# Sixty-four rows of a weight matrix through GpSimd's queue, and a reordered end of the last attention heads, in a decode kernel on one Trainium2 core

## The chip, the cores and the metric

The kernel runs on one core of one Trainium2 chip. The metric is device time in microseconds (us), the median of repeated executions. Kernels are compared only within the same rounds.

Ratios are the mean time of one kernel's fast runs over that of the other's of the same rounds, so a ratio is not quite the ratio of the medians that are quoted. The brackets hold a 95% interval.

## The reference

One decode step for 4 sequences: layer norm of x, then attention over a window of 2,048 cached keys in 32 heads of width 192, plus a gated feed-forward block on the same normalised input.

```python
W = min(4096, max(256, Sk // 4))                       # 2048
q = (xn @ wq).reshape(4, 1, 32, 192)                   # D = 640
scores = einsum("bhqd,bhkd->bhqk", q, k[last W]) * 192**-0.5
o = einsum("bhqk,bhkd->bhqd", softmax(scores), v[last W])
h = silu(xn @ w1) * (xn @ w3)                          # F = 1536
out = x + o.reshape(4, 1, 6144) @ wo + h @ w2
```

All data are bfloat16. K and V of the window are 201 of the 223 MB that have to be read once.

## The kernel before

Every head is one 3 MB K load and one 3 MB V load on SyncE's DMA queue. VectorE multiplies K by q, TensorE sums the products (`adder`), VectorE reduces them, a short chain over all engines gives the exponentials, VectorE spreads them into `z`, and TensorE multiplies z by V (`pv`). The result, divided by the sums and transposed, is `oT`, which TensorE multiplies by wo.

Two places matter here. The first is the load of w1, 640 rows of 1,536. The first 512 rows fill 128 partitions evenly. The next 64 rows are cut in halves, one half row for each partition, so that all 16 DMA engines share them (16 completion increments in the trace of before, 46.15 to 46.74 us, which I take as one an engine). The last 64 rows come as four small pieces into 12 partitions each.

```python
    KM, PH, LE, LI = KC - 1, P // 2, 3, 4               # 4, 64, 3, 4
    LP, LF, LB = LE * LI, CT + LE * LI, KM * P + PH      # 12, 44, 576
...
    def w1_load():
        w = B_w1
        wt = fpool.tile([P, FH + F], BF16, tag="w", name="w1")
        we = wopool.tile([LF, 2 * F], BF16, tag="wo", name="w1e")
        nc.gpsimd.memset(we[:], 0.0)
        nc.gpsimd.memset(wt[0:LF, FH:], 0.0)
        nc.sync.dma_start(out=wt[:, 0:FM], in_=w[0:KM * P, :].rearrange("(p kc) n -> p (kc n)", kc=KM))
        nc.sync.dma_start(out=wt[:, FM:FH], in_=w[KM * P:LB, :].rearrange("r (h n) -> (r h) n", h=2))
...
    def w1_low(n):                                      # four small pieces, 12 partitions each
        if n < 2:
            b0 = LB + n * 2 * LP
            nc.sync.dma_start(out=we[n * CT:n * CT + LP, :],
                              in_=w[b0:b0 + 2 * LP, :].rearrange("(i e s) n -> e i (s n)", e=LE, s=2))
...
```

The small pieces show the idea that the change extends. Their outer dimension is 3, and in the trace of before the first one has, after an increment soon after its issue, three completion increments (54.37 to 54.44 us) and not 16. I read this as three DMA engines: the piece gives those three more work, and the other 13 none.

The second place is the end. Slots of a schedule set the program order. Head 31 (the last, `H - 1`) has its chain and value product behind all of head 30's.

```python
    ends = {H - 2: (NU - 1, NU), H - 1: (NU + 3, NU + 4)}
    for h in range(H):
        u0, ul = h * GQ, h * GQ + GQ - 1
...
        for u in range(u0, ul + 1):
            add(u, 1, mult, u)
            add(u + 1, 2, adder, u)
            add(u + 1, 8, reduce_quarter, u)
        add(ul + 1, 9, chain_lmax, h)
        add(ul + 2, 3, chain_tr, h)
        add(ul + 2, 4, chain_gmax, h)
        add(ul + 3, 3, chain_bc, h)
        add(ul + 3, 4, chain_z, h)
        add(ul + 4, 5, ge_tot, h)
...
        v, m = ends.get(h, (u0 + L, u0 + L + 1))
        add(v, 7, pv, h)
        add(m, 7, ge_sum, h)
```

Of the kernel before, what the change touches and what calls it, by code (L numbers as in the profile page):

```python
# [10 lines left out]
FP32 = mybir.dt.float32  # L11
BF16 = mybir.dt.bfloat16
# [38 lines left out]
def kernel(  # L51
# [19 lines left out]
    nc = tc.nc  # L71
    P = 128
    B, Sq, D = A_x.shape
    _, H, Sk, Dh = A_k_cache.shape
    W = min(4096, max(256, Sk // 4))
    F = B_w1.shape[1]
# [129 lines left out]
    KM, PH, LE, LI = KC - 1, P // 2, 3, 4  # L206
    LP, LF, LB = LE * LI, CT + LE * LI, KM * P + PH
    assert D - LB == 5 * LP + LI and F % LE == 0
    xm = ppool.tile([B, 2, PH, 2], BF16, tag="pr", name="xm")
    nc.gpsimd.memset(xm[:], 0.0)  # L210
    for i in range(2):
        nc.vector.tensor_copy(out=xm[:, i, :, i], in_=xn[:, KM * P:LB])
    xe = ppool.tile([B, 3 + LE, LF], BF16, tag="pr", name="xe")
# [7 lines left out]
    for e in range(LE):  # L221
        nc.vector.tensor_copy(out=xe[:, 3 + e, CT + e * LI:CT + (e + 1) * LI], in_=xn[:, LB + 5 * LP:D])
    NX = KM + 2
    xw_ps = ps_t.tile([P, NX + 3 + LE, B], BF16, tag="t", name="xw_ps")
    for kc in range(KM):
        nc.tensor.transpose(out=xw_ps[:, kc, :], in_=xn[:, kc:KM * P:KM], identity=idb[0:B, 0:B])
    for i in range(2):
        nc.tensor.transpose(out=xw_ps[:, KM + i, :], in_=xm[:, i].rearrange("b r h -> b (r h)"), identity=idb[0:B, 0:B])
    for i in range(3 + LE):
        nc.tensor.transpose(out=xw_ps[0:LF, NX + i, :], in_=xe[:, i, :], identity=idb[0:B, 0:B])  # L230
    xw = const.tile([P, NX, NREP, B], BF16, name="xw")
    nc.vector.tensor_copy(out=xw[:], in_=xw_ps[:, 0:NX, :].unsqueeze(2).to_broadcast([P, NX, NREP, B]))
    xl = const.tile([LF, 3 + LE, NREP, B], BF16, name="xl")
    nc.vector.tensor_copy(out=xl[:], in_=xw_ps[0:LF, NX:, :].unsqueeze(2).to_broadcast([LF, 3 + LE, NREP, B]))

# [148 lines left out]
    FM, FH = KM * F, KM * F + F // 2  # L384

    def w1_load():
        w = B_w1
        wt = fpool.tile([P, FH + F], BF16, tag="w", name="w1")
        we = wopool.tile([LF, 2 * F], BF16, tag="wo", name="w1e")
        nc.gpsimd.memset(we[:], 0.0)  # L390
        nc.gpsimd.memset(wt[0:LF, FH:], 0.0)
        nc.sync.dma_start(out=wt[:, 0:FM], in_=w[0:KM * P, :].rearrange("(p kc) n -> p (kc n)", kc=KM))
        nc.sync.dma_start(out=wt[:, FM:FH], in_=w[KM * P:LB, :].rearrange("r (h n) -> (r h) n", h=2))
        ffn["w1"], ffn["w1e"] = wt, we

    def w1_low(n):
        w, wt, we = B_w1, ffn["w1"], ffn["w1e"]
        if n < 2:
            b0 = LB + n * 2 * LP
            nc.sync.dma_start(out=we[n * CT:n * CT + LP, :],  # L400
                              in_=w[b0:b0 + 2 * LP, :].rearrange("(i e s) n -> e i (s n)", e=LE, s=2))
        elif n == 2:
            nc.sync.dma_start(out=wt[0:LP, FH:FH + F], in_=w[LB + 4 * LP:LB + 5 * LP, :].rearrange("(i e) n -> e i n", e=LE))
        else:
            nc.sync.dma_start(out=wt[CT:LF, FH:FH + F // LE], in_=w[LB + 5 * LP:D, :].rearrange("i (e n) -> e i n", e=LE))

    def w1_in():
# [12 lines left out]
        for w in range(HG):  # L420
            c0 = FM + (w % 2) * FW
            mm(w, xw[:, KM + w // 2], wt[:, c0:c0 + FW])
        for i in range(2):
            for w in range(HG):
                mm(w, xl[:, i], we[:, i * F + w * FW:i * F + (w + 1) * FW])
        for w in range(HG):
            mm(w, xl[:, 2], wt[0:LF, FH + w * FW:FH + (w + 1) * FW])
        FE = F // LE
        for e in range(LE):
            for w in range(HG):  # L430
                c0, c1 = max(e * FE, w * FW), min((e + 1) * FE, (w + 1) * FW)
                if c0 < c1:
                    mm(w, xl[:, 3 + e], wt[0:LF, FH + c0 - e * FE:FH + c1 - e * FE], c0 - w * FW)
# [3 lines left out]
    def w3_load():  # L437
        wt = fpool.tile([P, KC, F], BF16, tag="w", name="w3")
        nc.sync.dma_start(out=wt[:].rearrange("p k n -> p (k n)"), in_=B_w3.rearrange("(p kc) n -> p (kc n)", kc=KC))
        ffn["w3"] = wt  # L440
# [33 lines left out]
    def add(slot, phase, fn, *args):  # L474
        sched[slot].append((phase, len(sched[slot]), fn, args))
# [3 lines left out]
    ends = {H - 2: (NU - 1, NU), H - 1: (NU + 3, NU + 4)}  # L479
    for h in range(H):  # L480
# [5 lines left out]
        for u in range(u0, ul + 1):  # L486
            add(u, 1, mult, u)
            add(u + 1, 2, adder, u)
            add(u + 1, 8, reduce_quarter, u)
        add(ul + 1, 9, chain_lmax, h)  # L490
        add(ul + 2, 3, chain_tr, h)
        add(ul + 2, 4, chain_gmax, h)
        add(ul + 3, 3, chain_bc, h)
        add(ul + 3, 4, chain_z, h)
        add(ul + 4, 5, ge_tot, h)
        if h % HG == HG - 1:
            add(ul + 4, 9, ge_rec, h // HG)
# [3 lines left out]
        if h % HG == HG - 1:  # L501
            add(m + 1, 0, ge_turn, h // HG)
    e = ends[H - 1][1] + 1
# [25 lines left out]
    add(e - 1, 8, ffn_out, 0)  # L529
# [44 lines left out]
```

## Time and profile before

| | before |
|---|---|
| time | 525.76 us (525.65 to 525.87, 3 runs) |
| span of the profiled run, mean granted clock | 523.8 us, 0.892 |
| bytes on the loads' queue | 222.96 MB |
| TensorE, VectorE busy | 69%, 65% |
| last w2 load landed | 520.75 us |

The first fence is from the profile page of before: the mean busy share of the DMA engines in 40 slices (in tenths), what they moved in GB/s, the queue of the loads, and the chain that ended last by engine.

```profile
DMA  9999999999999999999999999999999999999996
GB/s 389 422 443 425 433 431 432 428 433 432 430 435 428 437 418 446 424 437 426 434 434 429 432 434 429 435 427 435 425 437 434 427 437 431 430 434 425 441 418 275
...
q1 hardware_dynamic: 11868, 222.96, 99.2%
...
DMA 60%; PE 20%; DVE 15%; ACT 3%; issue 1%; SPq 1%
```

A share near 1.00 alone proves little: it counts time in which a packet was open. From 100 to 480 us the share is 1.00 at 432 GB/s. A packet of 24,576 bytes, one partition's part of a K or V load, takes 912 ns.

The end, from the timeline of TensorE of before (start and length in us, engine, line, operation, tiles, count; in brackets the idle time before it and what ended that):

```profile
513.30 2.71 PE L340 MATMUL o_ps<-vt,z 128*8 128x384 bf16 x32 [0.24 <-DVE z L332]
...
519.21 0.98 PE L264 MATMUL acc<-wo_t,oT 128*4 128x320 bf16 x12 [0.47 <-DMA wo_t<-in_A_wo_dram]
520.38 0.71 PE L264 MATMUL acc<-w,hT 128*4 128x320 bf16 x8 [0.19 <-DMA w<-in_B_w_dram]
```

The last two groups of products wait for loads, so the kernel ends with its DMA. The last w2 load has 16 completion increments, as many as there are DMA engines. Taken as one an engine, they show when each engine came to its end:

```
before, engine ends against 520.75 us: -3.2 -3.2 -3.0 -2.3 -1.9 -0.8 -0.8 -0.4 -0.3 -0.3 -0.3 -0.3 -0.3 -0.2 -0.1 0.0
mean of the 16: 519.68 us
```

Five engines are done 2 to 3 us early. Perfect balance would end all of them at their mean, 519.7 us, 1.1 us sooner. By this estimate that is all that balancing alone can win.

### The profile page before, as it was taken

The numbers are of one execution on the slowest core, as the hardware profiler recorded it, in microseconds if no ns is written. First come the engines' busy times: TensorE is split into PE (matmuls) and PEld (weight loads), VectorE is DVE, ScalarE is ACT, GpSimd is POOL, SyncE is SP. The second block draws the span as 40 slices with busy tenths as digits, with TensorE's granted clock in tenths as the row PEclk, the third lists the DMA queues.
The fourth block names the chain that finished last, engine by engine and source line by source line (L and its number), as shares of the span: only waits on it lengthen the run. The fifth ranks groups of instructions, "written<-read, shape, count | busy, mean of one in ns | idle before, by whom it ended". The sixth has DMA issues, their size and how long they took to land.

```text
span 523.8 us, 4820 instructions
## 1 busy us (share of the span) xinstructions
PE 361.8 (69%) x2336; PEld 75.9 (14%) x1643; DVE 340.9 (65%) x413; ACT 55.8 (11%) x176; POOL 5.6 (1%) x12
## 2 busy tenths in 40 slices
PE   0965866887668776667547768586686876675685
PEld 0100111121111111111111111111111111111122
DVE  3268853687656767577646877466667766667671
ACT  2111111111001110101100111001101110011111
POOL 4000000000000000000000000000000000000000
PEclk9979886898878998789997988889878898889988
DMA  9999999999999999999999999999999999999996
GB/s 389 422 443 425 433 431 432 428 433 432 430 435 428 437 418 446 424 437 426 434 434 429 432 434 429 435 427 435 425 437 434 427 437 431 430 434 425 441 418 275
DMA packets 11904, 223.26 MB, mean 426 GB/s; under 512 B 1332, under 2 KB 1608, under 8 KB 3052
## 3 DMA queue, kind: packets, MB, share of 16 engines
q1 hardware_dynamic: 11868, 222.96, 99.2%
q8 instruction: 15, 0.25, 0.2%
q14 instruction: 5, 0.04, 0.0%
q10 hardware_dynamic: 16, 0.01, 0.0%
HBM read 222.96 MB, written 0.01 MB: 426 GB/s over the span
## 4 chain that ended last, share of the span: by engine, by line
DMA 60%; PE 20%; DVE 15%; ACT 3%; issue 1%; SPq 1%
DMA kt<-in_A_k_cache_dram 44%; PE ps L288 11%; DMA w<-in_B_w_dram 11%; DVE pr L277 10%; DMA vt<-in_A_v_cache_dram 5%; PE po L361 4%; PE qps L243 3%; DVE sc L296 2%; ACT ex L324 1%; DVE z L332 1%; DMA x_sb<-in_A_x_dram 1%; PE mt L318 1%; ACT L324 0%; ACT negm L321 0%; PE mt L305 0%
## 5 line engine op out<-in xcount | busy, mean ns | idle before, releaser
L288 PE MATMUL ps<-pr,idb 128*128 128x512 bf16 x768 | 214.7, 422 | 137.6 <-DVE pr L277 137.5
L277 DVE TENSOR_TENSOR pr<-kt,qbc 128x3072 bf16<-128x3072 bf16 x128 | 223.5, 1746 | 104.0 <-DMA kt<-in_A_k_cache_dram 104.0
L296 DVE TENSOR_REDUCE sc<-ps 128x16 f32<-128x512 f32 x128 | 87.1, 681 | 2.7 <-PE ps L288 2.6
L340 PE MATMUL o_ps<-vt,z 128*8 128x384 bf16 x1024 | 60.5, 380 | 0.2 <-DVE z L332 0.2
L361 PE MATMUL po<-o_sb,sel_w 128*32 128x192 f32 x128 | 49.2, 518 | 0.6 <-ACT o_sb L343 0.6
L340 PEld LDWEIGHTS <-z 128*8 128x8 bf16 x1024 | 26.2, 95 | 98.8 <-issue 89.2
L332 DVE TENSOR_TENSOR z<-ex,mask_b 128x256 bf16<-128x256 bf16 x32 | 13.5, 423 | 38.6 <-ACT ex L324 38.6
L343 ACT COPY o_sb<-o_ps 128x384 f32<-128x384 f32 x32 | 15.3, 478 | 196.9 <-PE o_ps L340 196.9
L313 ACT ACTIVATE gneg<-gmax 1x128 f32<-1x128 f32 x32 | 9.8, 308 | 162.8 <-DVE gmax L310 162.8
L305 PEld LDWEIGHTS mt<-idf,lmax 128*1 128x1 f32 x32 | 3.2, 101 | 127.5 <-issue 125.5
L361 PEld LDWEIGHTS po<-o_sb,sel_w 128*32 128x32 f32 x128 | 13.8, 130 | 29.4 <-issue 27.9
L288 PEld LDWEIGHTS <-idb 128*128 128x128 bf16 x124 | 12.0, 97 | 39.3 <-issue 32.8
L318 PEld LDWEIGHTS mt<-ones_ff,gneg 1*128 1x128 f32 x64 | 9.6, 186 | 47.1 <-issue 43.7
L243 PE MATMUL qps<-wt,xnT 128*128 128x512 bf16 x59 | 14.9, 412 | 0.1
L318 PE MATMUL mt<-ones_ff,gneg 1*128 1x1 f32 x64 | 12.3, 259 | 0.7 <-ACT gneg L313 0.7
L321 ACT COPY negm<-mt 128x1 f32<-128x1 f32 x32 | 5.1, 159 | 70.4 <-PE mt L318 70.4
L310 DVE TENSOR_REDUCE gmax<-mt 1x4 f32<-1x128 f32 x32 | 8.8, 274 | 5.8 <-PE mt L305 5.8
L348 PEld LDWEIGHTS po<-rsum,tot_w 128*32 128x32 f32 x64 | 4.4, 108 | 51.5 <-ACT ex L324 35.4
L249 DVE CAST qbc<-qps 128x512 bf16<-128x512 f32 x6 | 3.8, 684 | 11.7 <-PE qps L243 11.7
L324 ACT ACTIVATE ex<-sc,negm 128x64 bf16<-128x64 f32 x32 | 11.1, 348 | 1.0
L305 PE MATMUL mt<-idf,lmax 128*1 128x128 f32 x32 | 10.9, 340 | 0.0
L199 PE MATMUL xnT_ps<-idb,xn 4*128 4x4 bf16 x5 | 0.4, 178 | 13.4 <-DVE xn L194 13.4
(74 smaller groups left out, 84.4 us busy)
## 6 DMA issues: line engine op xcount, KB each, us to landing
kt<-in_A_k_cache_dram SPq DMA_DIRECT2D x32, 3072.0 KB, 19.1
vt<-in_A_v_cache_dram SPq DMA_DIRECT2D x32, 3072.0 KB, 25.5
wo_t<-in_A_wo_dram SPq DMA_DIRECT2D x8, 960.0 KB, 20.7
wt<-in_A_wq_dram SPq DMA_DIRECT2D x2, 3072.0 KB
w<-in_B_w_dram SPq DMA_DIRECT2D x1, 1920.0 KB
wt<-in_A_wq_dram SPq DMA_DIRECT2D x1, 1536.0 KB, 19.5
w<-in_B_w_dram SPq DMA_DIRECT2D x1, 1536.0 KB
w<-in_B_w_dram SPq DMA_DIRECT2D x2, 640.0 KB
```

The source lines that it names most:

```text
L243: nc.tensor.matmul(qp[:], lhsT=xnT[:, kc].rearrange("p a b -> p (a b)"), rhs=wq_rows[kc][:, (c0 + i) * QC:(c0 + i + 1) * QC], start=(kc == ...
L277: nc.vector.tensor_tensor(out=pr[:], in0=kts[h][:, g * JQ:(g + 1) * JQ, :], in1=qbc[:, h * Dh:(h + 1) * Dh].unsqueeze(1).to_broadcast([P, ...
L288: nc.tensor.matmul(ps[:], lhsT=idb[:], rhs=pr[:, :, kk * DD:(kk + 1) * DD], start=(kk == 0), stop=(kk == NK - 1))
L296: nc.vector.tensor_reduce(out=scs[h][:, g * JQ:(g + 1) * JQ], in_=pss.pop(u)[:], axis=AX.X, op=ALU.add)
L305: nc.tensor.transpose(out=mt[0:1, 0:P], in_=chs[h][0][:], identity=idf[:])
L313: nc.scalar.activation(out=gneg[:], in_=gmax[:].unsqueeze(1).to_broadcast([1, PB, B]), func=ACTF.Copy, scale=-SCALE)
L318: nc.tensor.matmul(mt[:, P:P + 1], lhsT=gneg[:].rearrange("o p b -> o (p b)"), rhs=ones_ff[:], start=True, stop=True)
L324: nc.scalar.activation(out=ex[:], in_=scs.pop(h)[:], func=ACTF.Exp, bias=negm[:, 0:1], scale=SCALE, accum_out=rsum[:])
L332: nc.vector.tensor_tensor(out=z[:], in0=ex[:].unsqueeze(2).to_broadcast([P, NJ, B]), in1=mask_b[:].unsqueeze(1).to_broadcast([P, NJ, B]), ...
L340: nc.tensor.matmul(o_ps[c * CT:c * CT + 2 * B, :], lhsT=z[:, 2 * jj:2 * jj + 2, :], rhs=vt[:, 2 * jj:2 * jj + 2, :], start=(jj < 4), stop= ...
L343: nc.scalar.copy(out=o_sb[:], in_=o_ps[:])
L361: nc.tensor.matmul(po[sl, 0:Dh], lhsT=sel_w[:, par].rearrange("p a b -> p (a b)"), rhs=o_sb[:, par * Dh:(par + 1) * Dh].rearrange("p (r i) ...
```

## The change

Its intent has two parts.

- Loads: the 64 half rows no longer burden all engines. 24 rows and 40 rows are issued on GpSimd's queue as transfers with an outer dimension of 2, meant for one pair of engines each. Tiny transfers of 4, 1 and 7 rows (`skip`) are meant to move the place where GpSimd's queue takes its next engine, so that the pairs are engines 4 and 5, then 7 and 8. The destinations are partitions 16 to 23 and 60 to 67. Both the effect of the tiny transfers and the fit of these partitions to these engines were assumed: no trace had shown either.
- Tail: head 31's sums, largest score and exponentials stand ahead of head 30's value product where they can, and 25 matmuls whose results nobody reads fill TensorE's idle times.

```diff
-    LP, LF, LB = LE * LI, CT + LE * LI, KM * P + PH
+    LP, LF, LB = LE * LI, 68, KM * P
+    PA, PZ = 16, LF - GP                      # SA, SB, GP = 3, 5, 8
...
+    def skip(k):
+        t = const.tile([k, CT], BF16, name=f"skip{k}")
+        n = CT if k > 1 else CT - 1
+        nc.gpsimd.dma_start(out=t[:, 0:n], in_=B_w1[0:k, 0:n])
...
-        we = wopool.tile([LF, 2 * F], BF16, tag="wo", name="w1e")
-        nc.sync.dma_start(out=wt[:, FM:FH], in_=w[KM * P:LB, :].rearrange("r (h n) -> (r h) n", h=2))
+        we = vpool.tile([P, SB, F], BF16, tag="vt", name="w1e")
+        nc.gpsimd.memset(we[0:LF], 0.0)
+        for k, r0, p0, n in ((4, RA, PA, SA), (1, RB, PZ, SB)):
+            skip(k)
+            nc.gpsimd.dma_start(out=we[p0:p0 + GP, 0:n, :].rearrange("p s n -> p (s n)"),
+                                in_=B_w1[r0:r0 + n * GP, :].rearrange("(i e s) n -> e i (s n)", e=2, s=n))
+        skip(7)
...  # w3's load is cut in two; the products of w1's rows follow the new places
+    def warm(n):
+        for _ in range(n):
+            nc.tensor.matmul(ffn["warm"][:], lhsT=idb[:], rhs=qbc[:, 0:QC], start=True, stop=True)
...
-    ends = {H - 2: (NU - 1, NU), H - 1: (NU + 3, NU + 4)}
+    lastu = {NU - 2: (NU - 2, 1, NU - 2, 5), NU - 1: (NU - 2, 2, NU - 2, 6)}
+    ends = {H - 2: (NU - 1, NU - 0.4), H - 1: (NU, NU + 1)}
...
+        a, b, c, d = (ul + 1, ul + 2, ul + 3, ul + 4) if h < H - 1 else (NU - 1, NU - 0.5, NU - 0.2, NU)
...  # chain_lmax, chain_tr, chain_gmax, chain_bc, chain_z, ge_tot at a, b, b, c, c, d
+    add(NU - 3, 1.5, warm, 16)
+    add(NU - 0.3, 0, warm, 3)
+    add(NU - 0.1, 0, warm, 6)
```

More of the change, by code (lines that the diff above doesn't have):

```diff
@@ L201 @@
     nc.vector.tensor_copy(out=xnT[:], in_=xnT_ps[:].unsqueeze(2).to_broadcast([P, KC, PB, B]))
-    KM, PH, LE, LI = KC - 1, P // 2, 3, 4
-    LP, LF, LB = LE * LI, CT + LE * LI, KM * P + PH
-    assert D - LB == 5 * LP + LI and F % LE == 0
-    xm = ppool.tile([B, 2, PH, 2], BF16, tag="pr", name="xm")
-    nc.gpsimd.memset(xm[:], 0.0)
-    for i in range(2):
-        nc.vector.tensor_copy(out=xm[:, i, :, i], in_=xn[:, KM * P:LB])
-    xe = ppool.tile([B, 3 + LE, LF], BF16, tag="pr", name="xe")
+    KM, LE, LI, SA, SB, GP = KC - 1, 3, 4, 3, 5, 8
+    LP, LF, LB = LE * LI, 68, KM * P
+    PA, PZ = 16, LF - GP
+    RA = LB + 5 * LP + LI
+    RB = RA + SA * GP
+    assert RB + SB * GP == D and F % LE == 0
+    xe = ppool.tile([B, SB + LE, LF], BF16, tag="pr", name="xe")
     nc.gpsimd.memset(xe[:], 0.0)
@@ L221 @@
     for e in range(LE):
-        nc.vector.tensor_copy(out=xe[:, 3 + e, CT + e * LI:CT + (e + 1) * LI], in_=xn[:, LB + 5 * LP:D])
-    NX = KM + 2
-    xw_ps = ps_t.tile([P, NX + 3 + LE, B], BF16, tag="t", name="xw_ps")
+        nc.vector.tensor_copy(out=xe[:, SB + e, CT + e * LI:CT + (e + 1) * LI], in_=xn[:, LB + 5 * LP:RA])
+    for r0, p0, n in ((RA, PA, SA), (RB, PZ, SB)):
+        nc.vector.tensor_copy(out=xe[:, 0:n, p0:p0 + GP].rearrange("b s (e i) -> b s e i", e=2),
+                              in_=xn[:, r0:r0 + n * GP].rearrange("b (i e s) -> b s e i", e=2, s=n))
+    xw_ps = ps_t.tile([P, KM + SB + LE, B], BF16, tag="t", name="xw_ps")
     for kc in range(KM):
         nc.tensor.transpose(out=xw_ps[:, kc, :], in_=xn[:, kc:KM * P:KM], identity=idb[0:B, 0:B])
-    for i in range(2):
-        nc.tensor.transpose(out=xw_ps[:, KM + i, :], in_=xm[:, i].rearrange("b r h -> b (r h)"), identity=idb[0:B, 0:B])
-    for i in range(3 + LE):
-        nc.tensor.transpose(out=xw_ps[0:LF, NX + i, :], in_=xe[:, i, :], identity=idb[0:B, 0:B])
-    xw = const.tile([P, NX, NREP, B], BF16, name="xw")
-    nc.vector.tensor_copy(out=xw[:], in_=xw_ps[:, 0:NX, :].unsqueeze(2).to_broadcast([P, NX, NREP, B]))
-    xl = const.tile([LF, 3 + LE, NREP, B], BF16, name="xl")
-    nc.vector.tensor_copy(out=xl[:], in_=xw_ps[0:LF, NX:, :].unsqueeze(2).to_broadcast([LF, 3 + LE, NREP, B]))
+    for i in range(SB + LE):
+        nc.tensor.transpose(out=xw_ps[0:LF, KM + i, :], in_=xe[:, i, :], identity=idb[0:B, 0:B])
+    xw = const.tile([P, KM, NREP, B], BF16, name="xw")
+    nc.vector.tensor_copy(out=xw[:], in_=xw_ps[:, 0:KM, :].unsqueeze(2).to_broadcast([P, KM, NREP, B]))
+    xl = const.tile([LF, SB + LE, NREP, B], BF16, name="xl")
+    nc.vector.tensor_copy(out=xl[:], in_=xw_ps[0:LF, KM:, :].unsqueeze(2).to_broadcast([LF, SB + LE, NREP, B]))
     qbc = const.tile([P, H * Dh], BF16, name="qbc")
@@ L382 @@
     ffn = {}
-    FM, FH = KM * F, KM * F + F // 2
+    def skip(k):
+        t = const.tile([k, CT], BF16, name=f"skip{k}")
+        n = CT if k > 1 else CT - 1
+        nc.gpsimd.dma_start(out=t[:, 0:n], in_=B_w1[0:k, 0:n])
     def w1_load():
-        w = B_w1
-        wt = fpool.tile([P, FH + F], BF16, tag="w", name="w1")
-        we = wopool.tile([LF, 2 * F], BF16, tag="wo", name="w1e")
-        nc.gpsimd.memset(we[:], 0.0)
-        nc.gpsimd.memset(wt[0:LF, FH:], 0.0)
-        nc.sync.dma_start(out=wt[:, 0:FM], in_=w[0:KM * P, :].rearrange("(p kc) n -> p (kc n)", kc=KM))
-        nc.sync.dma_start(out=wt[:, FM:FH], in_=w[KM * P:LB, :].rearrange("r (h n) -> (r h) n", h=2))
-        ffn["w1"], ffn["w1e"] = wt, we
+        wt = fpool.tile([P, KM * F], BF16, tag="w", name="w1")
+        we = vpool.tile([P, SB, F], BF16, tag="vt", name="w1e")
+        nc.gpsimd.memset(we[0:LF], 0.0)
+        nc.sync.dma_start(out=wt[:], in_=B_w1[0:KM * P, :].rearrange("(p kc) n -> p (kc n)", kc=KM))
+        ffn["w1"], ffn["w1e"] = wt, we
+        for k, r0, p0, n in ((4, RA, PA, SA), (1, RB, PZ, SB)):
[3 more added lines that the diff above has]
+        skip(7)
     def w1_low(n):
-        w, wt, we = B_w1, ffn["w1"], ffn["w1e"]
+        w, we = B_w1, ffn["w1e"]
         if n < 2:
             b0 = LB + n * 2 * LP
-            nc.sync.dma_start(out=we[n * CT:n * CT + LP, :],
+            nc.sync.dma_start(out=we[n * CT:n * CT + LP, 0:2, :].rearrange("p s n -> p (s n)"),
                               in_=w[b0:b0 + 2 * LP, :].rearrange("(i e s) n -> e i (s n)", e=LE, s=2))
         elif n == 2:
-            nc.sync.dma_start(out=wt[0:LP, FH:FH + F], in_=w[LB + 4 * LP:LB + 5 * LP, :].rearrange("(i e) n -> e i n", e=LE))
+            nc.sync.dma_start(out=we[0:LP, 2, :], in_=w[LB + 4 * LP:LB + 5 * LP, :].rearrange("(i e) n -> e i n", e=LE))
         else:
-            nc.sync.dma_start(out=wt[CT:LF, FH:FH + F // LE], in_=w[LB + 5 * LP:D, :].rearrange("i (e n) -> e i n", e=LE))
+            nc.sync.dma_start(out=we[CT:CT + LP, 2, 0:F // LE], in_=w[LB + 5 * LP:RA, :].rearrange("i (e n) -> e i n", e=LE))
     def w1_in():
@@ L419, in w1_in @@
         main(0)
-        for w in range(HG):
-            c0 = FM + (w % 2) * FW
-            mm(w, xw[:, KM + w // 2], wt[:, c0:c0 + FW])
-        for i in range(2):
+        for i in range(SB):
             for w in range(HG):
-                mm(w, xl[:, i], we[:, i * F + w * FW:i * F + (w + 1) * FW])
-        for w in range(HG):
-            mm(w, xl[:, 2], wt[0:LF, FH + w * FW:FH + (w + 1) * FW])
+                mm(w, xl[:, i], we[0:LF, i, w * FW:(w + 1) * FW])
         FE = F // LE
@@ L432, in w1_in @@
                 if c0 < c1:
-                    mm(w, xl[:, 3 + e], wt[0:LF, FH + c0 - e * FE:FH + c1 - e * FE], c0 - w * FW)
+                    mm(w, xl[:, SB + e], we[0:LF, 2, c0 - e * FE:c1 - e * FE], c0 - w * FW)
         for kc in range(1, KM):
@@ L438, in w3_load @@
         wt = fpool.tile([P, KC, F], BF16, tag="w", name="w3")
-        nc.sync.dma_start(out=wt[:].rearrange("p k n -> p (k n)"), in_=B_w3.rearrange("(p kc) n -> p (kc n)", kc=KC))
+        for k0, k1 in ((0, KC - 2), (KC - 2, KC)):
+            nc.sync.dma_start(out=wt[:, k0:k1, :].rearrange("p k n -> p (k n)"),
+                              in_=B_w3.rearrange("(p kc) n -> p kc n", kc=KC)[:, k0:k1, :].rearrange("p k n -> p (k n)"))
         ffn["w3"] = wt
@@ L475, in add @@
         sched[slot].append((phase, len(sched[slot]), fn, args))
-    ends = {H - 2: (NU - 1, NU), H - 1: (NU + 3, NU + 4)}
+    def warm(n):
+        if "warm" not in ffn:
+            ffn["warm"] = ps_t.tile([P, QC], FP32, tag="t", name="warm")
+        for _ in range(n):
+            nc.tensor.matmul(ffn["warm"][:], lhsT=idb[:], rhs=qbc[:, 0:QC], start=True, stop=True)
+    lastu = {NU - 2: (NU - 2, 1, NU - 2, 5), NU - 1: (NU - 2, 2, NU - 2, 6)}
+    ends = {H - 2: (NU - 1, NU - 0.4), H - 1: (NU, NU + 1)}
     for h in range(H):
@@ L486 @@
         for u in range(u0, ul + 1):
-            add(u, 1, mult, u)
-            add(u + 1, 2, adder, u)
-            add(u + 1, 8, reduce_quarter, u)
-        add(ul + 1, 9, chain_lmax, h)
-        add(ul + 2, 3, chain_tr, h)
-        add(ul + 2, 4, chain_gmax, h)
-        add(ul + 3, 3, chain_bc, h)
-        add(ul + 3, 4, chain_z, h)
-        add(ul + 4, 5, ge_tot, h)
+            ms, mp, as_, ap = lastu.get(u, (u, 1, u + 1, 2))
+            add(ms, mp, mult, u)
+            add(as_, ap, adder, u)
+            add(min(u + 1, NU - 1), 8 if u != NU - 3 else 3, reduce_quarter, u)
+        a, b, c, d = (ul + 1, ul + 2, ul + 3, ul + 4) if h < H - 1 else (NU - 1, NU - 0.5, NU - 0.2, NU)
+        add(a, 9, chain_lmax, h)
+        add(b, 3, chain_tr, h)
+        add(b, 4, chain_gmax, h)
+        add(c, 3, chain_bc, h)
+        add(c, 4, chain_z, h)
+        add(d, 5, ge_tot, h)
         if h % HG == HG - 1:
-            add(ul + 4, 9, ge_rec, h // HG)
+            add(d, 9, ge_rec, h // HG)
         v, m = ends.get(h, (u0 + L, u0 + L + 1))
@@ L528 @@
     add(NU - 6, 0, w2_load, 3)
-    add(e - 1, 8, ffn_out, 0)
+    add(e - 1, 5, ffn_out, 0)
     add(e - 1, 8, ffn_out, 1)
```

## The prediction

> **What bounds it now.** The DMA engines. The page's DMA row is 9 in 39 of 40 slices (222.96 MB); in every window from 20 to 500 us the DMA share is 1.00 to 1.01, 430 to 434 GB/s. A 24,576-byte packet takes 912 ns and packets follow without gaps, so only each engine's load and the last engine's end matter. The chain of waits ends in the last w2 load (to 520.38), 0.76 us of TensorE, a 0.48 us copy and the output.
>
> The last transfer's 16 completion increments, one an engine, show imbalance: nine end between 520.37 and 520.75 us, two 0.8 early, five 3.2, 3.15, 2.95, 2.3 and 1.85 early. The lags start where three engines take w1's 12-partition pieces (four increments instead of 16) and move at instruction fetches: 15 packets of 16,384 bytes, 0.94 us each[...].
>
> **DMA.** The 64-row half-row load goes: 8 packets of 1,536 bytes on every engine, 65 ns each, with its semaphore 0.53 us. Splitting w3 gives back about 0.07, five GpSimd completions 0.05. Net -0.42 us everywhere. The rows return on two pairs: four pieces of 9,216 bytes (estimate 1.4 us) on each engine of one, four of 15,360 bytes (573 ns each, 2.3 us) of the other. [...] Five engines have 1.85 to 3.2 us of slack; if the pairs are among them, they end about 0.4 to 0.9 us before the front.
>
> **Tail.** Head 31's last quarter waits behind head 30's z: z is ready at 513.2 although v landed at 511.48; the value product takes 2.71 us against 1.47 elsewhere, at a granted clock of 0.56. wo's last product ends at 520.19, only 0.19 us before the awaited w2 piece, so the DMA gain alone would be worth only about 0.2 us. Summing head 31 early and keeping TensorE busy should bring z to about 509 to 510 and the product's end to 513, about 3 us earlier. That gain is hidden behind DMA; it lets the DMA gain through.
>
> **Off the path.** GpSimd's memset grows (2.65 us for 3,072 columns, estimate 6.6 for 7,680), ahead of loads needed at about 75 us. w1's remainder occupies a V buffer, so head 3's V load is issued after w1's products (82 us instead of 66); K is queued until 85 to 87 us. Any bubble falls on engines with slack.
>
> **Prediction.** 525.76 - 0.45 = 525.3 us, range 524.8 to 525.8. Faster by over 2%: 0.003; within 2%: 0.99; slower: 0.007.
>
> **What would show it.** Last w2 landing at about 520.3 instead of 520.75; its 16 increments' spread shrinking from 3.2 to 1 to 2 us, four engines moved towards the front; TensorE's last idle time still ended by DMA w2, wo's last product done before; head 31's value product starting near 511, taking about 1.5 us; DMA share still 1.00 from 80 to 90 us.
>
> **What would make it wrong.** [...] w1's products slip, the queue runs dry near 85 us: slower by 1 to 2 us. [...]

The forecast is 525.76 - 0.45 = 525.3 us, and 0.42 of the 0.45 are the loads' net: 0.53 for the half rows, less 0.07 and 0.05 (0.41 by the rounded terms). The packets bear these out: in before, eight of 65 ns (128 over 16 engines) and one 4-byte packet of 9 ns, which I take for the completion, make 0.53 us; in after, w3's pieces of 9,216 and 6,144 bytes take 347 and 234 ns, against 573 for one of 15,360 in before, which is 8 ns for each of eight and with one completion more 0.07 us; five completions of 9 ns are 0.05 us. The 1.4 us are the 573 ns scaled to 9,216 bytes, times four. That the rows would come on two pairs of engines with slack was the assumption.

What the forecast says of lags can be seen in before. The increments of the half-row load lie within 0.59 us (46.15 to 46.74), those of a load that ends after the first small pieces within 1.72 us (60.78 to 62.50). Each of the 15 instruction packets took 0.88 to 0.99 us, and for 14 of them a 24,576-byte packet that started within 0.02 us of their end took 1.37 to 1.46 us instead of 0.91. Taken as on the same engine, that is an estimate of about 1.4 us for each (0.94 for the packet and 0.5 for the one behind it). The forecast counted 0.94.

## More of the kernel before

The engines are full from the second slice to the last but one. The same in windows of before; the columns are the window, its length and busy time by engine (with counts), TensorE's granted clock, the DMA share and GB/s.

```profile
core 0: us, PE busy (x) PEld busy (x) DVE busy (x) ACT busy (x) POOL busy (x), PEclk, DMA share, GB/s
40.00:45.00 5.00, 3.24 (x16) 0.01 (x1) 4.96 (x6) 0.00 (x0) 0.00 (x0) 1.00 0.98 420
45.00:50.00 5.00, 3.35 (x17) 0.56 (x5) 3.83 (x4) 2.05 (x5) 0.00 (x0) 1.00 1.07 451
50.00:55.00 5.00, 2.57 (x9) 0.23 (x3) 3.40 (x5) 0.14 (x2) 0.00 (x0) 0.76 0.95 408
```

## The result, and the profile after

| | before | after |
|---|---|---|
| time, same chip, 4 runs each | 525.70 us (525.63 to 525.87) | 530.45 us (529.93 to 530.76) |
| ratio | | 1.0089 [1.0074, 1.0104] |
| span and clock of the profiled run | 523.8 us, 0.892 | 528.0 us, 0.903 |
| last w2 load landed | 520.75 us | 524.90 us |
| mean end of the 16 engines | 519.68 us | 522.24 us |
| output landed after the last w2 load | 2.22 us | 2.23 us |

The kernel became 4.7 us slower. The last load lands 4.15 us later, and everything behind it takes as long as before. The lines of the page of after that answer to those of before:

```profile
DMA  9999999999999999999999999999999999999995
GB/s 388 426 438 345 426 432 434 430 432 429 431 435 432 433 423 437 432 432 432 432 429 434 432 432 433 428 435 428 429 435 430 431 434 430 435 428 437 424 424 224
...
q1 hardware_dynamic: 11868, 222.76, 98.8%
q0 software_dynamic: 256, 0.20, 0.2%
...
DMA 63%; PE 19%; DVE 14%; ACT 2%; issue 1%; SPq 0%
```

The busy row is the same, but one slice, the fourth (39.6 to 52.8 us), moved 345 GB/s instead of 425. The missing 80 GB/s over 13.2 us are 1.06 MB, or 2.5 us at 430 GB/s. Windows of after:

```profile
40.00:45.00 5.00, 3.43 (x15) 0.00 (x0) 4.96 (x7) 0.00 (x0) 0.00 (x0) 0.99 1.03 370
45.00:50.00 5.00, 3.36 (x17) 0.57 (x5) 4.13 (x5) 1.75 (x3) 0.00 (x0) 1.00 1.04 300
50.00:55.00 5.00, 2.57 (x11) 0.23 (x3) 3.29 (x4) 0.44 (x2) 0.00 (x0) 0.88 0.96 403
```

The DMA share stays at 1.0 while the rate falls to 300 GB/s: the packets are open and crawl. The trace's packet records say which. The 16 data packets of GpSimd's queue run from 41.1 to 51.3 us. In that time 12,288-byte packets of w1's big load take up to 0.96 us instead of 0.46, and 24,576-byte packets of the K and V loads up to 1.9 us instead of 0.91. Between 35 and 55 us, 32 of the latter take over 1 us; in before it is one.

The engines' ends, and how the 4.15 us divide:

```
after, engine ends against 524.90 us: -5.3 -4.5 -4.3 -4.3 -4.0 -2.7 -2.7 -2.6 -2.6 -2.4 -2.4 -2.1 -1.4 -0.6 -0.5 0.0
mean end    519.68 -> 522.24   2.56 us   lost rate, shared by all engines
last - mean   1.07 ->   2.66   1.59 us   worse balance
```

Put in order, each of the 16 ends lies at least 1.9 us behind its counterpart in before, so the loss of rate reached every engine. The change lost on both counts: the 16 engines lost time together, and the balance that it was to mend became worse.

GpSimd's memset and the end, from the timelines of GpSimd and of TensorE of after:

```profile
28.99 6.49 POOL L392 MEMSET w1e<- 68x7680 bf16 x1 [26.65 <-PE qps L242]
```

```profile
515.11 0.82 PE L486 MATMUL warm<-qbc,idb 128*128 128x512 bf16 x3
515.86 0.38 PE L317 MATMUL mt<-ones_ff,gneg 1*128 1x1 f32 x2
...
517.65 1.46 PE L339 MATMUL o_ps<-vt,z 128*8 128x384 bf16 x29
...
523.38 0.98 PE L263 MATMUL acc<-wo_t,oT 128*4 128x320 bf16 x12 [1.35 <-DMA wo_t<-in_A_wo_dram]
524.54 0.71 PE L263 MATMUL acc<-w,hT 128*4 128x320 bf16 x8 [0.19 <-DMA w<-in_B_w_dram]
```

Head 31's value product takes 1.46 us for 29 of its 32 matmuls at a granted clock of 1.00 (517.65 to 519.11 us), against 2.71 us for all of them in before at 0.51 (513.30 to 516.01 us; the forecast's 0.56 is from 513.0 to 516.1). The last products still wait for their loads. But z of head 31 is no earlier against its keys: they land at 501.1 us and z is ready at 517.36, 16.3 us later. Before it was 496.97 and 513.24, also 16.3 us.

### The profile page after: what moved, and what is told of

Read it like the earlier page. It is cut to its first block, busy times and chain, and to the rows that moved or that the text cites. A ratio compares the mean times of both kernels' runs of the same rounds, so it can differ in the third digit from the quotient of the medians.

```text
span 528.0 us, 4861 instructions
## 1 busy us (share of the span) xinstructions
PE 362.4 (69%) x2366; PEld 75.7 (14%) x1648; DVE 339.6 (64%) x413; ACT 55.8 (11%) x176; POOL 10.8 (2%) x15
## 4 chain that ended last, share of the span: by engine, by line
DMA 63%; PE 19%; DVE 14%; ACT 2%; issue 1%; SPq 0%
DMA kt<-in_A_k_cache_dram 47%; PE ps L287 11%; DVE pr L276 9%; DMA w<-in_B_w_dram 6%; DMA w1e<-in_B_w_dram 5%; DMA vt<-in_A_v_cache_dram 5%; PE po L360 4%; PE qps L242 3%; DVE sc L295 2%; ACT ex L323 1%; DMA x_sb<-in_A_x_dram 1%; DVE z L331 1%; PE mt L317 1%; PE f_ps L417 0%; PE mt L304 0%
## 5 line engine op out<-in xcount | busy, mean ns | idle before, releaser
L339 PE MATMUL o_ps<-vt,z 128*8 128x384 bf16 x1024 | 55.7, 356 | 0.0
L342 ACT COPY o_sb<-o_ps 128x384 f32<-128x384 f32 x32 | 15.3, 478 | 191.9 <-PE o_ps L339 191.9
L263 PE MATMUL acc<-wo_t,oT 128*4 128x320 bf16 x96 | 9.2, 298 | 1.3 <-DMA wo_t<-in_A_wo_dram 1.3
## 6 DMA issues: line engine op xcount, KB each, us to landing
wt<-in_A_wq_dram SPq DMA_DIRECT2D x2, 3072.0 KB, 16.3
```

The lines of the kernel that those rows point to most:

```text
L339: nc.tensor.matmul(o_ps[c * CT:c * CT + 2 * B, :], lhsT=z[:, 2 * jj:2 * jj + 2, :], rhs=vt[:, 2 * jj:2 * jj + 2, :], start=(jj < 4), stop= ...
L342: nc.scalar.copy(out=o_sb[:], in_=o_ps[:])
```

## The experiments

All kernels gave correct results. Twelve were run. Two questions lead: which half of the change costs the time, and why all engines slow down while a few small transfers run.

### The tail alone

The loads of before with the schedule of after (five rounds; before on that chip 526.08 us).

```diff
 # after, with w1_load, w1_low, w1_in, w3_load and their x tiles as in before
```

> The tail part alone (head 31 ahead, unread matmuls), with the loads of before. If the loss of 4.7 us is all in the loads, this is within 0.3 us of before (525.4 to 525.9), the last w2 load landing at about 520.7, and head 31's value product takes about 1.5 us instead of 2.71. If the tail itself costs anything, it is slower than 526.5.

Measured: 526.88 us (526.35 to 527.37), ratio 1.0018 [1.0004, 1.0031]. So the first branch of the expectation was missed, and the second holds: the tail itself costs something. The last load landed at 520.81 us, as in before, but the output landed 2.73 us after it instead of 2.22. The timeline of TensorE of this run:

```profile
498.17 3.63 PE L484 MATMUL warm<-qbc,idb 128*128 128x512 bf16 x16
501.64 1.46 PE L288 MATMUL ps<-pr,idb 128*128 128x512 bf16 x6
...
513.07 0.82 PE L484 MATMUL warm<-qbc,idb 128*128 128x512 bf16 x3
513.82 0.38 PE L318 MATMUL mt<-ones_ff,gneg 1*128 1x1 f32 x2
...
520.13 0.98 PE L264 MATMUL acc<-wo_t,oT 128*4 128x320 bf16 x12 [0.92 <-DVE oT L369]
520.95 0.71 PE L264 MATMUL acc<-w,hT 128*4 128x320 bf16 x8
```

Head 31's first products were ready at 498.7 us, but their sum starts at 501.64, behind 16 unread matmuls. The broadcast of the largest score (L318) could start near 511.9 us. It starts at 513.82, behind head 30's last sum and three more unread ones. The last wo product now waits for oT and not for its load. So the tail part alone costs 0.5 us by the landing of the output and 0.9 us by the mean times (0.2 to 1.6 us by the interval). In after this is hidden, because there the loads come 4 us later.

### The loads alone

The loads of after with the schedule of before (three rounds).

```diff
 # after, with lastu, warm and the a, b, c, d slots taken out, and ends as in before
```

> The load part alone, with the tail order of before. If the loads hold the whole loss: 529.5 to 531 us, the window from 40 to 53 us again near 350 GB/s instead of 430, last w2 landing near 524.9. If the loss comes from the two parts together, it is clearly below 529.

Measured: 530.05 us (529.64 to 530.11), ratio 1.0076 [1.0062, 1.0090]; 368, 313 and 398 GB/s in the three windows; last landing 524.72 us. The loads hold the loss.

### Six tiny transfers of two rows

My first reading, which this run refuted, was that the place is kept apart for each number of engines, so that transfers of 4, 1 and 7 partitions don't move it for the pairs. Six transfers of two partitions each, two before the rows and four after, should then give engines 4 and 5, then 6 and 7. What this and later expectations call "ports", then "foreign partitions", is a theory under test: rows that go into partitions which another engine fills in the big loads slow all engines. "Ports" is only its name, and no trace shows which engine fills which partitions; the choice of destinations is an assumption throughout.

```diff
-        for k, r0, p0, n in ((4, RA, PA, SA), (1, RB, PZ, SB)):
-            skip(k)
+        skip(0)                       # each now 2 partitions
+        skip(1)
+        for r0, p0, n in ((RA, PA, SA), (RB, PZ, SB)):      # PZ = 56
...
-        skip(7)
+        for k in range(2, 6):
+            skip(k)
```

> GpSimd's queue still carries the 64 rows, but with dummies of two rows each (two ahead, four behind) and partitions 16 to 23 and 56 to 63. My reading of the trace of after is that [...]the rows fell on engines 0 to 3; with two dummies of k=2 they should fall on engines 4, 5 and 6, 7[...]. Theory 'ports' (rows written by an engine other than the partitions' own slow every engine): no slow window, 430 GB/s from 40 to 53 us, spread of the last landing about 1 to 2.5 us, 525.0 to 525.8 us. Theory 'software queue' (any data through GpSimd's queue slows all engines): window still near 350 GB/s, about 528 to 530 us.

Measured: 530.16 us (530.01 to 530.33), ratio 1.0080 [1.0066, 1.0094]; 350, 327 and 389 GB/s; last landing 524.85 us. Nothing moved: the packets of the 24 rows start in step with those of the engines that I call 0 and 1, the packets of the 40 rows with those of 2 and 3, as in after. My reading of how the tiny transfers count fell here.

### The same rows and partitions on SyncE's queue

Is it GpSimd's queue? The same two pieces, with the same destinations, were issued by SyncE. In the trace each then has two completion increments after the one at issue (48.49 and 48.57 us for the first), and of the three engines of w1's next small piece two end 3.5 us behind the third (57.52, 60.99, 61.06 us; 54.37 to 54.44 in before). So the rows are on two of those three; I call these two engines 0 and 1, and the three 0 to 2.

```diff
-            skip(k)
-            nc.gpsimd.dma_start(out=we[p0:p0 + GP, 0:n, :]...
+            nc.sync.dma_start(out=we[p0:p0 + GP, 0:n, :]...          # partitions 16-23 and 60-67
```

> The same two row pieces to the same partitions (16 to 23, 60 to 67), but issued on SyncE's queue without dummies: two engines (0 and 1, as with k=3 on 0 to 2) write them all. Theory 'ports': a slow window again while they are written, loads below 400 GB/s for some 8 us, total above 527 (imbalance 3 us and the slow window). Theory 'software queue': every window stays at 430 GB/s, and only imbalance is left: those two engines carry 3.7 us more, last landing about 524, total about 528 to 529. The window's GB/s decides, not the total.

Measured: 532.61 us (532.13 to 533.74), ratio 1.0129 [1.0116, 1.0143]; last landing 527.10 us. The windows of this run:

```profile
40.00:45.00 5.00, 3.02 (x13) 0.18 (x2) 4.97 (x6) 0.00 (x0) 0.00 (x0) 1.00 0.95 408
45.00:50.00 5.00, 3.37 (x16) 0.62 (x6) 3.65 (x6) 2.19 (x5) 0.00 (x0) 1.00 1.13 276
50.00:55.00 5.00, 2.69 (x10) 0.04 (x8) 2.86 (x3) 0.00 (x0) 0.00 (x0) 0.70 0.93 306
```

The slow stretch is there without any GpSimd transfer, and worse. So it is not the queue. What after and this run have in common is the rows' partitions, 16 to 23 and 60 to 67, and that the first engines carry the rows (0 to 3, and 0 and 1).

### SyncE's queue, partitions 32 to 39 and 0 to 7

The next theory: an engine that writes into partitions which another engine is filling at full rate slows all of them. So the rows, still on engines 0 and 1, now go to partitions 32 to 39 and 0 to 7. The choice rests on an assumption about which engine fills which partitions in a big load; the run shows only what the change of partitions does.

```diff
-    PA, PZ = 16, LF - GP
+    PA, PZ = 32, 0                    # and columns 3 to 7 of w1e, LF = 44
```

> As e4_hw_cross, SyncE's queue and engines 0 and 1, but the two pieces go to partitions 32 to 39 and 0 to 7[...] (five more slots of the w1e tile, 12 more matmuls). Theory 'ports' (an engine that writes partitions which another engine fills at full rate slows all): no slow window, 425 GB/s or more from 45 to 55 us where e4 had 276 and 306; only the two engines' extra 3.7 us of load remains, last landing about 524, total about 529. Rival 'shape' (a transfer of long pieces on two engines slows all loads wherever it writes): the window stays below 330 GB/s, total about 532 to 533.

Measured: 529.20 us (528.76 to 530.37), ratio 1.0073 [1.0057, 1.0090]; last landing 523.71 us. Windows:

```profile
40.00:45.00 5.00, 3.37 (x15) 0.08 (x1) 4.96 (x6) 0.00 (x0) 0.00 (x0) 1.00 0.99 423
45.00:50.00 5.00, 3.35 (x16) 0.49 (x4) 3.66 (x4) 2.19 (x5) 0.00 (x0) 1.00 1.03 439
50.00:55.00 5.00, 2.57 (x9) 0.23 (x3) 3.29 (x4) 0.00 (x0) 0.00 (x0) 0.82 1.05 452
```

The slow stretch is gone. The engines end at 520.19 us in the mean, against 523.08 in the run above. What is left is mostly imbalance: two engines carry all the 64 rows, and the other 14 end at least 1.6 us before either. The mean end is still 0.5 us behind before's, for which no run gives a reason.

### GpSimd's queue, partitions 32 to 39 and 8 to 15

The same for GpSimd: issue and tiny transfers as in after, so the rows come from engines 0 to 3 again, and other destinations: 32 to 39, and 8 to 15, chosen by the same assumption.

```diff
-    PA, PZ = 16, LF - GP
+    PA, PZ = 32, 8                    # and columns 3 to 7 of w1e, LF = 44; after's tail
```

> GpSimd's queue with the dummies of 4, 1 and 7 rows as in after, but the rows' destinations follow the engines where I read them in the trace (24 rows on engines 0 and 1, 40 rows on 2 and 3): partitions 32 to 39 and 8 to 15. Theory 'ports': no slow window; engine 2, which w1's other pieces load too, carries 2.3 us more and ends last: landing 522.6 or so, total about 527.5. If GpSimd's queue slows the loads whatever it writes, or if I misread the engines: window near 320 GB/s again, total about 530.

Measured: 527.05 us (526.97 to 527.43), ratio 1.0027 [1.0012, 1.0042]; last landing 522.06 us, mean end 519.80 us. Windows:

```profile
40.00:45.00 5.00, 3.27 (x16) 0.14 (x2) 4.97 (x6) 0.00 (x0) 1.49 (x3) 1.00 1.00 425
45.00:50.00 5.00, 3.35 (x16) 0.43 (x4) 3.65 (x5) 2.19 (x5) 0.00 (x0) 1.00 1.03 436
50.00:55.00 5.00, 2.57 (x9) 0.23 (x3) 3.21 (x4) 0.00 (x0) 0.00 (x0) 0.79 1.05 447
```

With the engines, the tiny transfers and the tail of after kept and the destinations changed, the mean end is back near before's (519.68). What stays is 1.2 us of imbalance: these engines also carry w1's small pieces.

### A probe of GpSimd's engine choice

The kernel before, with 16 tiny transfers of different widths on GpSimd's queue, some with one row for each engine and some with several, and marks of 2, 4 and 6 partitions on SyncE's queue to compare with. The results are not used; a packet's size tells which transfer it belongs to. Two readings were to be told apart: each transfer on two engines takes another pair than the one before it, or the place moves only after some of them.

```diff
+        for j, (parts, e) in enumerate(((2, None), (2, None), (8, 2), (2, None), (8, 2), ... (16, 4), ...)):
+            probe(nc.gpsimd, parts, 53 if parts == 1 else 50 + 4 * j, e)      # e: several rows an engine
...
+        for k in (2, 4, 6):
+            probe(nc.sync, k, 130 + 4 * k)
```

> Before, with sixteen tiny transfers on GpSimd's queue, each of its own size (100 to 1200 bytes a row; 1, 2, 4, 7, 8 and 16 partitions), written to a scratch tile that nobody reads, and three tiny ones on SyncE's queue on 2, 4 and 6 engines as marks. The sizes tell in the packet records which engines each took. [...] No slow window in either case (tiny amounts); time within 0.5 us of before if tiny transfers on GpSimd's queue cost nothing.

Measured: 526.24 us in a single run; 419, 441 and 428 GB/s. The trace's packet records do not name the engine. In before 16 packets of more than 4 bytes are open in 94% of the time from 100 to 480 us, as many as there are engines, so I take it that an engine has one of them at a time. Two packets that start the same few ns apart as two packets of a mark are then read as being on the same engines. The numbers are names: those of the mark of 2 I call 0 and 1, those of the mark of 4, 0 to 3:

| transfer on GpSimd's queue | engines |
|---|---|
| 2 partitions, one row each, at 8 places in the order | always 0, 1: 13 to 21 ns apart, the mark's 13 |
| 2 partitions, one row each, the last two | not told: 0.34 us apart, and no mark near them |
| 4 partitions, one row each | 0 to 3: the last two 0.227 us apart, as in the mark of 4 |
| 8 partitions as 2 x 4 rows, the first such | 0, 1 |
| 8 partitions as 2 x 4 rows, the second | 2, 3: 0.227 us apart, as these two in the mark of 4 |
| 16 partitions as 4 x 4 rows, the third | four further ones |

So in the probe the transfers with one row for each engine that could be read (8 of two partitions, and the one of 4) started at engine 0 and did not move the place. Those with several rows took the next engines (0 and 1, then 2 and 3, then four further ones), and moved it. Read in the same way, the three `skip`s of after moved nothing: 24 rows went to engines 0 and 1, 40 rows to 2 and 3. The trace of after agrees: the three engines of w1's first small piece, level within 0.1 us in before, end at 58.01, 58.30 and 58.93 us.

### The change with its tiny transfers repaired

After as it is, both parts, with one thing mended: the tiny transfers have two rows for each engine, so that they count (4; then 3, 7, 7; then 7). Destinations stay as in after. By counting on from engine 0, and past the 16th from 0 again, the rows should now come from engines 4 and 5, 7 and 8. These numbers are reckoned so here and below; no trace names them, and none shows the step past the 16th.

```diff
-        t = const.tile([k, CT], BF16, name=f"skip{k}")
-        nc.gpsimd.dma_start(out=t[:, 0:n], in_=B_w1[0:k, 0:n])
+        nc.gpsimd.dma_start(out=pad[0:2 * k, c0:c0 + n], in_=B_w1[0:2 * k, 0:n].rearrange("(i e) n -> e i n", e=k))
...
-        for k, r0, p0, n in ((4, RA, PA, SA), (1, RB, PZ, SB)):
+        for ks, r0, p0, n in (((4,), RA, PA, SA), ((3, 7, 7), RB, PZ, SB)):
```

> The change as it stands, tail included, with one repair: the tiny transfers have two rows for each engine (4; then 3, 7, 7; then 7 engines), because the probe showed that only transfers with several rows an engine move the place where GpSimd's next transfer starts. So the 24 rows should come from engines 4 and 5[...] and the 40 rows from engines 7 and 8[...]. Theory 'foreign partitions' (an engine that writes into partitions which another engine is filling slows all of them): no slow window, about 425, 437 and 445 GB/s in 40-45, 45-50 and 50-55 us, last load landing near 520.3 us; the time is then set by the tail, as in the run of the tail alone: 526.2 us (525.6 to 526.8). Rival 'the GpSimd queue's rows cost this wherever they go': slow windows below 400 GB/s and 530 us.

Measured: 526.95 us (526.33 to 527.28), ratio 1.0016 [1.0004, 1.0029]; before on that chip 525.74. Windows:

```profile
40.00:45.00 5.00, 3.37 (x15) 0.00 (x0) 4.97 (x7) 0.00 (x0) 0.00 (x0) 1.00 1.00 423
45.00:50.00 5.00, 3.35 (x17) 0.57 (x5) 4.07 (x4) 1.80 (x4) 0.00 (x0) 1.00 1.02 429
50.00:55.00 5.00, 2.57 (x11) 0.23 (x3) 3.29 (x4) 0.39 (x2) 0.00 (x0) 0.86 1.07 458
```

This is the cleanest pair: the same rows, the same queue, the same destinations as in after, other engines. (The tiny transfers differ too, but those of after also stand in the run before the probe, which has no slow stretch.) The slow stretch is gone, and the mean end is 519.78 us instead of 522.24. The three engines of w1's first small piece are level again (54.04 to 54.19 us), so I take it that the rows have left them. A 15,360-byte packet of the rows takes 0.57 us; in after it took 0.71 to 1.38. The one size that I missed is the last landing, 521.46 us and not 520.3: one engine ends 1.1 us behind all others. That, and not the tail, sets the time: the last wo product waits for its load again, and not for oT.

### Repaired loads, before's tail

```diff
 # the repaired loads, with the schedule of before
```

> The repaired loads with the tail of before. Foreign partitions: no slow window, last landing 520.2 to 520.6 us against 520.75, time 0.1 to 0.4 us below before, some 525.4 us. If the engines 4, 5, 7 and 8 are not the ones with slack, the last landing is later, 521 to 522, and the time 526 to 527. Rival (GpSimd's queue as such): 530 us.

Measured: 526.51 us (525.46 to 527.14), ratio 1.0011 [0.9998, 1.0024]; last landing 521.23 us, mean end 519.82. The loss of rate is gone here too (406, 437 and 446 GB/s), and the gain that was left does not come: one engine is 0.6 us behind the rest.

### Repaired loads, mended tail

```diff
-    ends = {H - 2: (NU - 1, NU - 0.4), H - 1: (NU, NU + 1)}
+    ends = {H - 2: (NU - 1, NU - 0.1), H - 1: (NU, NU + 1)}     # head 30's last sum behind the broadcast
-    add(NU - 3, 1.5, warm, 16)
-    add(NU - 0.3, 0, warm, 3)
-    add(NU - 0.1, 0, warm, 6)
+    add(NU - 0.5, 9, warm, 3)
```

> The repaired loads with a mended tail: the 16 unread matmuls ahead of head 31's first sums and the 9 later ones are out (3 are left while the largest score is being found), and head 31's broadcast of the maximum stands ahead of head 30's last sum in TensorE's order, which then fills the wait for the exponentials. If it was the unread matmuls and that order that kept z of head 31 at 16.3 us after its keys had landed, z comes 3 to 4 us earlier, near 512 us, the last wo products wait for their load again and not for oT, and the time is 525.3 us (525.0 to 525.7). Rival (the order of head 31's sums was never free to be earlier, VectorE sets it): z still at 515 us and 526.2 us.

Measured: 526.65 us (526.20 to 527.18), ratio 1.0013 [1.0001, 1.0026]; last landing 521.29 us. The timeline of TensorE of this run:

```profile
510.39 0.38 PE L317 MATMUL mt<-ones_ff,gneg 1*128 1x1 f32 x2
510.70 1.19 PE L360 MATMUL po<-o_sb,sel_w 128*32 128x192 f32 x3
...
512.07 1.47 PE L339 MATMUL o_ps<-vt,z 128*8 128x384 bf16 x32
...
519.76 0.98 PE L263 MATMUL acc<-wo_t,oT 128*4 128x320 bf16 x12 [1.33 <-DMA wo_t<-in_A_wo_dram]
520.93 0.71 PE L263 MATMUL acc<-w,hT 128*4 128x320 bf16 x8 [0.19 <-DMA w<-in_B_w_dram]
```

Head 31's keys land at 497.5 us, and z is ready at 511.9: 14.4 us later, against 16.3 in before and in after and 18.4 in the tail alone. On the same repaired loads it was 17.3 us with after's tail and 15.3 with before's, so the mended tail itself wins 0.9 us over before's. Unread matmuls and the order had held z back. The value product takes 1.47 us without 22 of the 25 unread ones, about as in after with all of them, since head 30's last sum fills the wait. The order of the tail does what it should, but the time does not move, because the end waits for the loads.

### Forty rows on engines 6 and 7

```diff
-    LP, LF, LB = LE * LI, 68, KM * P
+    LP, LF, LB = LE * LI, 64, KM * P        # the 40 rows into partitions 56-63, no tiny transfer between; before's tail
```

> As the repaired loads with before's tail, but the 40 rows go to the pair of engines that follows the first, 6 and 7, and into the partitions 56 to 63[...]; one tiny transfer for four engines ahead, one for eight behind. Foreign partitions: no slow window, and a time that differs from the run with engines 7 and 8 only by how much slack engine 6 has against engine 8: 525.4 us if it has as much, up to 1.5 us more if it has none. Rival: 530 us.

Measured: 527.29 us (527.24 to 528.33), ratio 1.0034 [1.0020, 1.0047]; last landing 522.32 us, mean end 519.78; no slow stretch (417, 445 and 441 GB/s). Two engines are behind here, the last by 2.0 us against the third last and the other by 1.0.

### Forty rows on 4 and 5, twenty-four on 7 and 8

```diff
-        for ks, r0, p0, n in (((4,), RA, PA, SA), ((3, 7, 7), RB, PZ, SB)):
+        for ks, r0, p0, n in (((4,), RB, PA, SB), ((3, 7, 7), RA, PZ, SA)):
```

> The repaired loads with the mended tail, and the two groups of rows changed over: the 40 rows go to engines 4 and 5 and into partitions 16 to 23, the 24 rows to engines 7 and 8 and into 60 to 67. In the three placed runs every load ran at full rate and the mean end of the engines was 519.8 us (before: 519.7), but one engine ended 0.6 to 1.1 us behind all others, and with engines 6 and 7 for the 40 rows two did. Reading: engine 7 had less slack than the 2.3 us that 40 rows cost it. Then here, with 1.4 us for engine 7 instead, the last engine is no more than 0.9 us behind the mean, the last landing is 520.5 to 520.8 us instead of 521.3, and the time is 525.4 to 525.9 us, which is before's within what can be told. Rival (the straggler is set by later instruction fetches, whatever rows an engine had): again one engine 0.6 to 1.1 us behind, last landing 521.2 or later, 526.5 us. Neither expects a gain that could be told from zero: what the rows free on the other engines is the 0.46 us of one 12,288-byte packet.

Measured: 527.63 us (526.42 to 528.51), ratio 1.0036 [1.0022, 1.0049]; before 525.70; last landing 522.05 us, mean end 519.75, no slow stretch. Both readings missed. One engine is now 1.7 us behind all others. My guess that engine 7 lacked slack fell; the straggler grew when engines 4 and 5 got more. The rival, that instruction fetches set the straggler, isn't excluded: I didn't follow on which engines they fell. (The expectation also misnames what the rows free on each engine: it is eight packets of 1,536 bytes, 65 ns each, 0.52 us.)

The five placed runs agree with one reading, by the engine numbers as reckoned: one engine of the pair 4 and 5 had no slack, so that 24 rows put it 0.6 to 1.1 us behind and 40 rows, 0.9 us more work, 1.7 us; engine 6 had none either. Which of the two it is, no run tells. No version beat before.

### All of them in one table

The last landing in the profiled run against the time gained or lost (ratio less 1, times 525.7 us):

| kernel | engines of the 24; 40 rows\*\* | their partitions | slow packets* | mean end | last landing against before | time against before |
|---|---|---|---|---|---|---|
| before | | | 1 | 519.68 | | |
| after | 0, 1; 2, 3 | 16-23; 60-67 | 32 | 522.24 | +4.15 | +4.7 |
| tail alone | | | 2 | 519.71 | +0.06 | +0.9 |
| loads alone | as after | 16-23; 60-67 | 42 | 522.21 | +3.97 | +4.0 |
| six of two rows | 0, 1; 2, 3 | 16-23; 56-63 | 46 | 522.37 | +4.10 | +4.2 |
| SyncE, same partitions | 0, 1 | 16-23; 60-67 | 67 | 523.08 | +6.35 | +6.8 |
| SyncE, other partitions | 0, 1 | 32-39; 0-7 | 1 | 520.19 | +2.96 | +3.8 |
| GpSimd, other partitions | 0, 1; 2, 3 | 32-39; 8-15 | 1 | 519.80 | +1.31 | +1.4 |
| repaired, after's tail | 4, 5; 7, 8 | 16-23; 60-67 | 1 | 519.78 | +0.71 | +0.8 |
| repaired, before's tail | 4, 5; 7, 8 | 16-23; 60-67 | 0 | 519.82 | +0.48 | +0.6 |
| repaired, mended tail | 4, 5; 7, 8 | 16-23; 60-67 | 1 | 519.83 | +0.54 | +0.7 |
| 40 rows on 6 and 7 | 4, 5; 6, 7 | 16-23; 56-63 | 0 | 519.78 | +1.57 | +1.8 |
| changed over | 7, 8; 4, 5 | 60-67; 16-23 | 1 | 519.75 | +1.30 | +1.9 |

\* 24,576-byte packets that took over 1 us, of the 216 to 278 recorded between 35 and 55 us.

\*\* Engines 0 to 3 as read from the starts of packets and the completion increments, the later ones as reckoned.

The four kernels whose rows came on engines 0 to 3 into partitions between 16 and 23 and between 56 and 67 have 32 to 67 slow packets. With the same engines and other partitions, or the same partitions and other engines, none has more than one, and the tail alone has two. Where the loads were changed the time goes with the last landing, at most 0.9 us above it; the tail alone, whose end waits for oT, is the exception.

## Why the prediction was wrong

The prediction said 525.3 us, and the change ran in 530.45 us, outside its range. The chance given to "within 2%" was borne out, but that says little for a change of 0.9%.

- **That the tiny transfers of 4, 1 and 7 rows set the engines of the rows: the step that failed.** They moved nothing: in the probe only transfers with several rows for each engine did, and these have one. The 24 and 40 rows fell on engines 0 to 3 instead of 4, 5, 7 and 8. The probe showed it, and in the repaired kernel the three engines of w1's first small piece were level again. I had noted that no trace showed it and then built the estimate on it.
- **The consequence was not in the sum at all.** I costed misplaced rows as imbalance alone, up to 1.9 us by an estimate (the 2.3 us of the 40 rows less the 0.42 gained would give it). Imbalance was 1.59 us of the 4.15 us by which the last load came later. The larger term, 2.56 us in the mean end, was rate lost by all 16 engines: 64 rows (0.20 MB of 223 MB) took it down to 276 to 327 GB/s from 45 to 50 us in the four kernels with slow packets, where before moved 451. It was shown from both sides: other partitions for the same engines cured it (mean end 522.24 to 519.80 us, and 523.08 to 520.19 on SyncE's queue), and so did other engines for the same partitions (522.24 to 519.78). That fits the theory that a few engines wrote into partitions that others were filling, but no trace shows who fills which. The big loads fill all partitions all the time, so whether such writes would cost anything where no other engine writes was not tested. Why engines that have nothing to do with the rows slow down is not shown either.
- **"Last w2 landing at about 520.3".** This was wrong also where the rows were placed as meant: 521.2 to 521.5 us, one engine 0.6 to 1.1 us behind. The gain on the other engines was there ("-0.42 us everywhere"): in the repaired kernel the sixth to the fifteenth of the ends in order come 0.2 to 0.4 us sooner than in before. I knew that five engines had slack, but not which ones. "If the pairs are among them" was the honest form; the number took the if as given.
- **"Bring z to about 509 to 510".** Wrong. Relative to its keys, z was not earlier at all in after (16.3 us), and 2.1 us later in the tail alone, where 16 unread matmuls stood ahead of real sums. The shorter value product (2.71 to about 1.5 us, a factor of 1.8, at granted clocks of 0.51 and 1.00) was right. But in the mended tail it took 1.47 us with three unread matmuls.
- **"Hidden behind DMA".** Right in after, and in all runs with the repaired loads. Not in the tail alone, where oT came last and cost about 0.6 us.
- **DMA-bound; memset; V buffer.** Right in what mattered: the memset took 6.49 us (estimate 6.6), and no queue ran dry (DMA share 1.02 at 435 GB/s from 80 to 90 us). Head 3's V load was issued at 75.25 us, later than before's 65.95, but not at the 82 forecast.

The experiments leave open which of engines 4 and 5 had no slack. They also leave open whether the 0.5 us that the rows free could be won with a better choice of engines. It would be 0.1% of the time, which five rounds with an interval of about 0.13% to either side cannot tell from nothing.

## What to carry to other kernels

A DMA share of 1.00 is not a rate (it was 1.04 at 300 GB/s in after): read the GB/s and the length of a known packet beside it. If a transfer uses only some engines, its destination partitions can cost the time of all: here the mean end came 2.4 and 2.9 us sooner when the rows went to other partitions (522.24 to 519.80 us on GpSimd's queue, 523.08 to 520.19 on SyncE's), and 2.5 us sooner with other engines (519.78). So try other partitions, and check in the trace which engines it really got before resting anything on it. Before filling idle time of an engine with unread work, look at what stands behind it in program order: in the tail alone 16 unread matmuls held a sum until 501.64 us whose products were ready at 498.7.
